# Expert layers: the row scatters of the output lose their order among each other

## The chip, the cores and the metric

The kernel runs on one core of one Trainium2 chip. The metric is the device time of one launch in microseconds (us), as the median of several runs; smaller is better. Engines are named as in the profile: PE is TensorE's matmul stream and PEld its weight loads, DVE is VectorE, ACT is ScalarE, POOL is GpSimd and SP is SyncE, which here only issues transfers.

## The reference

The first half is a gated linear attention over 4 x 8 heads of 768 steps with 48 channels each. The second half takes its 3072 output rows of 384 numbers as tokens and sends each through one of eight expert networks:

```python
def _moe_ref(x, modality_id, w_gate, modality_bias, w1, w2):
    N, D = x.shape                       # 3072, 384
    E = w_gate.shape[1]                  # 8
    logits = x @ w_gate + modality_bias[modality_id]
    e_idx = np.argmax(logits, axis=1)
    ...                                  # probs: softmax of the logits
    gate_w = probs[np.arange(N), e_idx]
    out = np.zeros((N, D), dtype=np.float32)
    for e in range(E):
        mask = e_idx == e
        h = np.maximum(x[mask] @ w1[e], 0.0)          # w1[e]: 384 x 1024
        out[mask] = gate_w[mask, None] * (h @ w2[e])  # w2[e]: 1024 x 384
    return out
```

Each token has exactly one expert, so each row of the output is written exactly once.

## The kernel before

The attention half (`gate_loop`, lines 23 to 280) fills a DRAM tensor `x_rows` with the 3072 rows in bf16 and an on-chip table `lg` with the gate logits. Beside it `cast_weights` writes bf16 copies of the expert weights, `w1b` and `w2b`, to DRAM. None of this is touched.

`moe_sorted` (lines 294 to 505) is the expert half. Lines 305 to 438 work out which expert each token goes to and give every token a slot, so that tokens of one expert stand together in tiles of 256 slots (two halves of 128). There are 12 tiles that always run and up to 7 more that run under a condition on their number (`nt`, line 499); with these inputs 13 tiles run. The table `idg` says which row of `x_rows` fills a slot, `ids` which row of `out` a slot's result goes to (an unfilled slot has an index beyond the last row, which the transfer drops).

One tile `i` goes through four functions:

- `fetch(i)`: two plain transfers on SP's queue bring the expert's weights, `w1t` (line 444) and `w2t` (line 445), 768 KB each, and two indirect transfers issued by POOL gather 128 rows each into `xg` (line 449). Weights have 3 buffers each, `xg` has 6, which is three tiles' worth of either.
- `turn`: PE transposes the gathered rows (line 457), DVE copies them to `xgT` (line 459).
- `up`: 24 matmuls into `h_ps` (line 469); the relu to `hT` is done in four pieces, two by DVE (line 471) and two by ACT (line 473).
- `down`: per half, 8 matmuls into `y_ps` (line 481), then one instruction that multiplies by the gate weight into `y_sb` (ACT for the first half, line 484; DVE for the second, line 486), then one indirect transfer issued by POOL that scatters the 128 rows of `y_sb` to `out` (line 487). `y_sb` has 4 buffers, two tiles' worth.

The written order is: fetch the next tile, `up` of this one, `turn` of the next one, `down` of this one. Every engine runs its own queue in order; the order in each queue is fixed when the kernel is built and may differ from the written one, as the gathers on POOL's queue do. Waits between instructions are derived from which tiles and tensors they read and write. A buffer of `y_sb` is written again only when the scatter that reads it has landed. All scatters write the tensor `out` at rows known only at run time, so each of them is ordered behind the one before it.

The last tile (line 505, index 12) stands in a conditional block behind line 499, which loads the number of tiles into each engine's registers.

Of the kernel before, what the change touches and what calls it, by code (L numbers as in the profile page):

```python
# [293 lines left out]
def moe_sorted(nc, ctx, tc, cpool, identb, lg, x_rows, w1b, w2b, moe_modality_id, moe_modality_bias, out):  # L294

    N, Dt = out.shape
# [140 lines left out]
    ids = mp.tile([128, NH], U32, name="ids")  # L437
# [38 lines left out]
    def down(i, w2t, hT):  # L476
        for s in range(HS):
            c = i * HS + s
            y_ps = pp.tile([128, Dt], F32, name="y_ps", tag="y", bufs=2)
            for f in range(NF):  # L480
                nc.tensor.matmul(y_ps[:], hT[:, f, s * 128:(s + 1) * 128], w2t[:, f, :], start=(f == 0), stop=(f == NF - 1))  # L481
            y_sb = fp.tile([128, Dt], F32, name="y_sb", bufs=4)
            if s % 2 == 0:
                nc.scalar.activation(y_sb[:], y_ps[:], Act.Copy, scale=inv[:, 1, c:c + 1])
            else:
                nc.vector.tensor_scalar(y_sb[:], y_ps[:], inv[:, 1, c:c + 1], None, Alu.mult)  # L486
            nc.gpsimd.indirect_dma_start(out=out, out_offset=bass.IndirectOffsetOnAxis(ap=ids[:, c:c + 1], axis=0), in_=y_sb[:], in_offset=None, bounds_check=N - 1, oob_is_err=False)  # L487


    got = fetch(0)  # L490
# [1 line left out]
    for i in range(NL):  # L492
        coming = fetch(i + 1)
        hT = up(got[0], xgT)
        if i + 1 < NL:
            xgT = turn(coming[2])
        down(i, got[1], hT)
        got = coming
    nt = nc.values_load(ntile[0:1, 0:1], min_val=NL, max_val=NS, skip_runtime_bounds_check_because="N tokens in at most E tiles that are not full")  # L499
    with ExitStack() as more:  # L500
        for i in range(NL, NS):
            more.enter_context(tc.If(nt > i))
            if i > NL:
                got = fetch(i, "n")
            down(i, got[1], up(got[0], turn(got[2])))
# [72 lines left out]
```

## Time and profile before

| | |
|---|---|
| median of 3 runs | 619.71 us (612.57 to 619.93) |
| the profiled execution, its own time | 614.6 us |
| its span, first to last instruction | 612.7 us |
| instructions | 10055 |
| PE busy | 397.7 us, 65% of the span |
| DVE busy | 354.4 us, 58% |
| ACT busy | 266.7 us, 44% |
| POOL busy | 82.7 us, 13% |
| mean granted TensorE clock | 0.851 of full |

The shares are means over the whole span, in which the attention half takes the larger part. The expert tiles begin at 482.75 us, with the first gather, and the last scatter is issued at 606.49 us. What bears on this change is read from that stretch alone.

### The profile page before, as it was taken

The numbers are of one execution on the slowest core, as the hardware profiler recorded it, in microseconds if no ns is written. First come the engines' busy times: TensorE is split into PE (matmuls) and PEld (weight loads), VectorE is DVE, ScalarE is ACT, GpSimd is POOL, SyncE is SP. The second block draws the span as 40 slices with busy tenths as digits, with TensorE's granted clock in tenths as the row PEclk, the third lists the DMA queues.
The fourth block names the chain that finished last, engine by engine and source line by source line (L and its number), as shares of the span: only waits on it lengthen the run. The fifth ranks groups of instructions, "written<-read, shape, count | busy, mean of one in ns | idle before, by whom it ended". The sixth has DMA issues, their size and how long they took to land. (4 is left out here: it accounts for less than half of the span.)

```text
span 612.7 us, 10055 instructions
## 1 busy us (share of the span) xinstructions
PE 397.7 (65%) x3656; PEld 292.1 (48%) x3656; DVE 354.4 (58%) x884; ACT 266.7 (44%) x597; POOL 82.7 (13%) x144
## 2 busy tenths in 40 slices
PE   0022122129799978987987999999914695876670
PEld 0011011117566656665656767776604574654450
DVE  1899999988876587588871444444365142232120
ACT  3556756475745574476652444444410031211120
POOL 5112000000000000000000000000000343435322
PEclk9999999999755685588996999999955599887886
DMA  9999998365652364353525445444217177765610
GB/s 201 234 243 267 261 254 218 116 175 117 172 151 74 93 159 127 87 154 99 134 70 114 88 93 105 91 98 99 50 12 305 32 269 254 255 230 184 206 53 28
DMA packets 108405, 91.49 MB, mean 149 GB/s; under 512 B 73342, under 2 KB 97314, under 8 KB 108352
## 3 DMA queue, kind: packets, MB, share of 16 engines
q1 hardware_dynamic: 93920, 70.94, 41.7%
q0 software_dynamic: 14432, 19.86, 15.7%
q8 instruction: 31, 0.51, 0.4%
q14 instruction: 22, 0.18, 0.1%
HBM read 86.75 MB, written 29.59 MB: 190 GB/s over the span
## 5 line engine op out<-in xcount | busy, mean ns | idle before, releaser
L111 PE MATMUL tq<-ident,Qh 128*96 128x128 f32 x192 | 42.9, 390 | 119.2 <-DVE Qh L107 119.2
L111 PEld LDWEIGHTS tq<-ident,Qh 128*96 128x96 f32 x192 | 31.3, 180 | 128.2 <-ACT g L76 62.0
L219 PE MATMUL py<-KW,V 96*64 96x192 f32 x512 | 88.9, 378 | 0.0
L185 DVE TENSOR_TENSOR KW<-wp,mask 96x384 f32<-96x384 f32 x64 | 35.3, 553 | 78.5 <-PE wp L184 67.0
L143 DVE TENSOR_TENSOR x<-e,an 128x192 f32<-128x192 f32 x192 | 67.7, 353 | 2.5
L184 PE MATMUL wp<-QT,KT 96*64 96x96 f32 x1024 | 65.8, 287 | 0.8 <-ACT KT L178 0.5
L184 PEld LDWEIGHTS wp<-QT,KT 96*64 96x64 f32 x1024 | 58.5, 165 | 5.6 <-ACT KT L178 4.3
L469 PE MATMUL h_ps<-xgT,w1t 128*128 128x256 bf16 x312 | 42.6, 296 | 25.2 <-DVE hT L471 22.0
L473 ACT ACTIVATE hT<-h_ps 128x512 bf16<-128x512 f32 x26 | 15.5, 597 | 97.5 <-PE h_ps L469 97.5
L150 DVE TENSOR_TENSOR e<-x 128x96 f32<-128x96 f32 x190 | 48.0, 253 | 2.7
L469 PEld LDWEIGHTS <-w1t 128*128 128x128 bf16 x312 | 32.8, 105 | 33.3 <-issue 26.3
L173 POOL MEMSET KT<- 96x256 f32 x32 | 10.9, 365 | 275.0 <-PE wp L184 275.0
L223 PE MATMUL py<-QT,Zs 96*48 96x96 f32 x448 | 37.5, 272 | 14.1 <-ACT Zs L209 14.1
L177 PE MATMUL tk<-ident,KW 96*96 96x96 f32 x256 | 40.1, 298 | 9.4 <-DMA KW<-kh 8.9
L219 PEld LDWEIGHTS py<-KW,V 96*64 96x64 f32 x512 | 39.6, 154 | 10.4 <-issue 2.4
L486 DVE TENSOR_SCALAR y_sb<-y_ps,inv 128x384 f32<-128x384 f32 x13 | 8.0, 617 | 60.9 <-DMA out_dram<-y_sb,ids 48.0
L112 ACT COPY QT<-tq 96x512 f32<-96x512 f32 x48 | 27.5, 582 | 34.9 <-PE tq L111 34.7
L481 PE MATMUL y_ps<-w2t,hT 128*128 128x384 bf16 x208 | 40.5, 353 | 0.0
L223 PEld LDWEIGHTS py<-QT,Zs 96*48 96x48 f32 x448 | 26.7, 136 | 26.9 <-ACT Zs L209 22.7
L209 ACT COPY Zs<-tz 96x512 f32<-96x512 f32 x28 | 16.3, 582 | 48.5 <-PE tz L207 48.5
L177 PEld LDWEIGHTS tk<-ident,KW 96*96 96x96 f32 x256 | 28.5, 154 | 17.6 <-issue 10.4
L178 ACT COPY KT<-tk 96x384 f32<-96x384 f32 x64 | 29.2, 477 | 16.9 <-PE tk L177 16.1
(120 smaller groups left out, 700.6 us busy)
## 6 DMA issues: line engine op xcount, KB each, us to landing
w1t<-w1b SPq DMA_DIRECT2D x13, 768.0 KB, 5.0
w2t<-w2b SPq DMA_DIRECT2D x13, 768.0 KB, 5.5
kh<-e SPq DMA_DIRECT2D x24, 384.0 KB, 2.9
KW<-kh SPq DMA_DIRECT2D x32, 288.0 KB, 3.7
w1b<-in_moe_w_dram POOLq DMA_DIRECT2D x8, 768.0 KB, 43.8
w2b<-in_moe_w_dram POOLq DMA_DIRECT2D x8, 768.0 KB, 46.4
cB<-c_scr SPq DMA_DIRECT2D x56, 96.0 KB, 3.4
ab<-in_a_re_dram SPq DMA_DIRECT2D x24, 192.0 KB, 5.3
```

Of the source, the lines that this page charges most:

```text
L111: nc.tensor.transpose(tp[:, i, :], Qh[:, t4 + i].rearrange("p c d -> p (c d)"), ident[:])
L112: nc.scalar.copy(QT[:, :, c * T + t4:c * T + t4 + 4], tp.rearrange("c t p -> c p t"))
L143: nc.vector.tensor_tensor(x[:], E[c][:, i, :, None, :].broadcast_to([P, 2, 2, D]), an[:, i].rearrange("p (u w) d -> p u w d", u=2), Alu.mult)
L150: nc.vector.tensor_tensor(to, x[:, 0], x[:, 1], Alu.add)
L177: nc.tensor.transpose(tp[:, i, :], KW[:, h4 + i, 0:C], ident[:L, :L])
L178: nc.scalar.copy(KT[:, h4:h4 + 4, 0:L], tp[:])
L184: nc.tensor.matmul(wp[u * 64:(u + 1) * 64, i, :], KT[:, h4 + i, u * 64:(u + 1) * 64], QT[:, p, :], start=True, stop=True)
L185: nc.vector.tensor_tensor(KW[:, h4:h4 + 4, C:], wp[0:L], mask[:, None, :].broadcast_to([L, 4, L]), Alu.mult)
L219: nc.tensor.matmul(py[u * 64:(u + 1) * 64, i, :], V[:, 2 * j + u, :], KW[:, 2 * j + u, :], start=True, stop=(g == 0))
L223: nc.tensor.matmul(py[u * 64:u * 64 + D, i, C:], Zs[:, j, u * 64:u * 64 + D], QT[:, p, :], start=False, stop=True)
L469: nc.tensor.matmul(h_ps[:, f, :], w1t[:, k, ff * 128:(ff + 1) * 128], xgT[:, k, :], start=(k == 0), stop=(k == KD - 1))
L481: nc.tensor.matmul(y_ps[:], hT[:, f, s * 128:(s + 1) * 128], w2t[:, f, :], start=(f == 0), stop=(f == NF - 1))
```

## The change

Each scatter is declared to have no dependence on the other members of a group named "scatter", and is then added to that group. The scatter itself, its operands, its place in the code and the number of instructions written are the same. The order between a scatter and the instruction that fills its `y_sb`, and between a scatter and the next writer of that buffer, is not part of the declaration.

```diff
@@ -484,7 +484,10 @@
                 nc.scalar.activation(y_sb[:], y_ps[:], Act.Copy, scale=inv[:, 1, c:c + 1])
             else:
                 nc.vector.tensor_scalar(y_sb[:], y_ps[:], inv[:, 1, c:c + 1], None, Alu.mult)
-            nc.gpsimd.indirect_dma_start(out=out, out_offset=bass.IndirectOffsetOnAxis(ap=ids[:, c:c + 1], axis=0), in_=y_sb[:], in_offset=None, bounds_check=N - 1, oob_is_err=False)
+
+            sc = nc.gpsimd.indirect_dma_start(out=out, out_offset=bass.IndirectOffsetOnAxis(ap=ids[:, c:c + 1], axis=0), in_=y_sb[:], in_offset=None, bounds_check=N - 1, oob_is_err=False)
+            tc.declare_no_dep(sc.ins, group="scatter", reason="rows of different tokens")
+            tc.add_to_no_dep_group("scatter", sc.ins)
```

## Rows read from the trace of the kernel before

**Rows 1.** The span in 40 slices: busy tenths of PE, POOL; granted clock.

```profile
PE   0022122129799978987987999999914695876670
POOL 5112000000000000000000000000000343435322
PEclk9999999999755685588996999999955599887886
```

**Rows 2.** Chain that ended last: start us, us, what.

```profile
600.24 2.57 DMA out_dram<-y_sb,ids
...
603.59 2.13 DMA out_dram<-y_sb,ids
...
606.49 0.97 POOL out_dram L487
```

**Rows 3.** POOL in order of time: start us, us, instruction [idle before <-releaser].

```profile
482.75 1.05 POOL L449 DMA_INDIRECT xg<-x_rows,idg  x1 [37.23 <-DVE empty L436]
...
494.17 0.95 POOL L449 DMA_INDIRECT xg<-x_rows,idg  x1 [0.30 <-PE y_ps L481]
495.42 1.03 POOL L487 DMA_INDIRECT out_dram<-y_sb,ids  x1 [0.30 <-issue]
502.66 1.00 POOL L487 DMA_INDIRECT out_dram<-y_sb,ids  x1 [6.21 <-DVE hT L471]
...
606.49 0.97 POOL L487 DMA_INDIRECT out_dram<-y_sb,ids  x1 [1.94 <-DMA out_dram<-y_sb,ids]
```

**Rows 4.** Waits, 482 to 613 us: us in total, times, longest.

```profile
DVE y_sb L486 <- DMA out_dram<-y_sb,ids: 48.0, 8, 9.0
POOL out_dram L487 <- DMA out_dram<-y_sb,ids: 30.9, 10, 5.8
PE h_ps L469 <- DVE hT L471: 22.0, 5, 6.3
```

**Rows 5.** DVE and PE around 519 us, in order of time.

```profile
519.18 0.62 DVE L486 TENSOR_SCALAR y_sb<-y_ps,inv 128x384 f32<-128x384 f32 x1 [8.96 <-DMA out_dram<-y_sb,ids]
519.72 1.28 DVE L471 TENSOR_SCALAR hT<-h_ps 128x512 bf16<-128x512 f32 x2
520.45 1.44 PE L469 MATMUL h_ps<-xgT,w1t 128*128 128x256 bf16 x6 [6.25 <-DVE hT L471]
```

**Rows 6.** PE and DVE, tiles 1 to 3 and 11, in order of time.

```profile
495.15 2.78 PE L469 MATMUL h_ps<-xgT,w1t 128*128 128x256 bf16 x24
...
495.35 0.62 DVE L486 TENSOR_SCALAR y_sb<-y_ps,inv 128x384 f32<-128x384 f32 x1 [2.04 <-PE y_ps L481]
...
500.71 2.78 PE L469 MATMUL h_ps<-xgT,w1t 128*128 128x256 bf16 x24
500.91 0.62 DVE L486 TENSOR_SCALAR y_sb<-y_ps,inv 128x384 f32<-128x384 f32 x1 [2.04 <-PE y_ps L481]
...
506.26 3.04 PE L469 MATMUL h_ps<-xgT,w1t 128*128 128x256 bf16 x24
...
581.78 2.88 PE L469 MATMUL h_ps<-xgT,w1t 128*128 128x256 bf16 x24
```

**Rows 7.** PE and DVE, end of tile 11 and tile 12, in order of time.

```profile
584.50 2.76 PE L481 MATMUL y_ps<-w2t,hT 128*128 128x384 bf16 x16
...
589.24 0.62 DVE L486 TENSOR_SCALAR y_sb<-y_ps,inv 128x384 f32<-128x384 f32 x1 [4.60 <-DMA out_dram<-y_sb,ids]
590.10 0.56 DVE L459 COPY xgT<-xg_ps 128x768 bf16<-128x768 bf16 x1 [0.24 <-DVE y_sb L486]
590.71 4.21 PE L469 MATMUL h_ps<-xgT,w1t 128*128 128x256 bf16 x24 [3.11 <-DVE xgT L459]
...
597.56 0.62 DVE L486 TENSOR_SCALAR y_sb<-y_ps,inv 128x384 f32<-128x384 f32 x1 [2.56 <-PE y_ps L481]
```

**Rows 8.** Lines 449 and 487: duration ns min/median/max; below it line 487's landing.

```profile
L449 POOL DMA_INDIRECT xg<-x_rows,idg x26: 943/962/1047, 482.8 to 574.4; - x26
L487 POOL DMA_INDIRECT out_dram<-y_sb,ids x26: 971/999/1032, 495.4 to 606.5; - x26
DMA to landing us min/median/max: 2.1/3.2/6.4
```

**Rows 9.** Stretches: us, busy by engine (x), PEclk, DMA share, GB/s.

```profile
495.00:500.50 5.50, 5.50 (x47) 4.24 (x46) 2.56 (x4) 1.78 (x3) 1.15 (x2) 1.00 0.95 337
511.90:526.30 14.40, 8.14 (x49) 5.38 (x47) 2.37 (x4) 2.36 (x4) 6.36 (x7) 0.76 0.61 209
563.90:569.40 5.50, 5.50 (x47) 4.24 (x46) 2.56 (x4) 1.19 (x2) 1.67 (x2) 1.00 0.82 264
598.20:612.70 14.50, 0.00 (x0) 0.00 (x0) 0.00 (x0) 0.00 (x0) 2.92 (x3) 0.58 0.09 30
```

**Rows 10.** SP's issues of weights: last before the expert tiles, first in them.

```profile
461.79 0.33 SPq L445 DMA_DIRECT2D w2t<-w2b  x1
492.58 0.34 SPq L444 DMA_DIRECT2D w1t<-w1b  x1
```

## The prediction

> **What bounds the kernel now.** I read the slices first, to find the stretch in which the scatters run: POOL is idle from slice 5 to slice 30 and works only in the last nine, and there PE falls from nines to sixes and lower, with its granted clock down as well [rows 1]. So PE is not what limits this stretch all the time.
>
> Then the chain of waits, to see what sets the end. It is scatter, landing, scatter: the last three are issued 3.35 and 2.90 us apart while nothing else runs [rows 2]. POOL's own timeline shows that this holds from the start. Ten gathers are issued back to back from 482.75 to 494.17 us, one every 1.27 us; then the scatters begin, and the second is issued 7.24 us after the first though its `y_sb` was written by 495.97 us [rows 3, 6] (the row blames DVE, but what was still under way was the first scatter). From the second, at 502.66, to the last, at 606.49, the 26 scatters need 103.83 us for 24 steps, 4.33 us each, 8.65 us for the two of a tile [rows 3].
>
> The table of waits tells who pays: POOL waits 30.9 us for a landing by name, DVE 48.0 us before it may write `y_sb` again, and PE 22.0 us for DVE's `hT` [rows 4]. One place shows how these hang together: DVE stands 8.96 us at line 486 for a buffer of `y_sb`; the relus of line 471 are queued behind it; PE gets `h_ps` back only then, after 6.25 us idle [rows 5]. A late scatter thus stalls DVE, DVE stalls PE, and PE comes back at the lower clock (1.44 us for 6 matmuls, against 2.78 us for 24 at full clock [rows 5, 6]).
>
> How fast the tiles go where no scatter holds them is seen at the start: the `up` matmuls of tiles 1, 2 and 3 begin at 495.15, 500.71 and 506.26 us, 5.56 us apart, at a granted clock of 1.00, the level of 2.4 GHz [rows 6, 9]. That is PE's own pace: it is busy for 5.50 of 5.50 us. Tile 11 begins at 581.78, so the ten steps from tile 1 took 86.63 us, 8.66 each [rows 6], which is the scatters' 8.65.
>
> **The change, part by part.** It adds no instruction to the work. It removes one wait for each of 25 scatters, that for the landing of the one before. What is left for a scatter is its `y_sb` and POOL's queue.
>
> *Tiles 1 to 11.* At PE's pace ten steps are 10 x 5.56 = 55.6 us against 86.63: 31.0 us less. The saving includes the clock, since the pace is that of full clock, and PE has no idle time left in which to lose it.
>
> *From tile 11 to tile 12.* Before, 590.71 - 581.78 = 8.93 us. There the last `y_sb` write of tile 11 stands ahead of `xgT` on DVE, and it waited 4.60 us for a landing [rows 7]. Without that it starts right behind the end of `down` at 584.50 + 2.76 = 587.26 (0.04 us behind, as in tile 1 [rows 6]: 500.91), takes 0.62, `xgT` follows 0.24 later, takes 0.56, and PE starts 0.05 after it: 588.77, so 6.99 us: 1.9 less.
>
> *Tile 12.* From the first `up` matmul to the end of the last `y_sb`, 598.18 - 590.71 = 7.47 us, with `up` at 4.21 us, the lower clock, after 3.11 us idle. PE would now idle about 1.2 us before it. No row shows whether the clock survives that. Bounds: nothing, or 4.21 - 2.78 = 1.4 us less. I take nothing, since the row of this very place is the nearest, and keep 1.4 for the range.
>
> *Last `y_sb` to last scatter.* Before, 606.49 - 598.18 = 8.31 us, a backlog of three scatters [rows 3, 7]. Now POOL has only its own queue: the scatter of the first half is just done, and 0.30 us lie between two of POOL's instructions, so some 0.6 us: 7.7 less. From there to the end of the span (612.7 - 606.49 = 6.2 us) nothing changes.
>
> The sum is 31.0 + 1.9 + 0 + 7.7 = 40.6 us. Against the profiled execution's own 614.6 us that gives 574. This execution lies between the runs shown, whose median is 5.1 us above it; the four times shown have a mean of 616.7, and off that I get **576 us**.
>
> **What covers what, and what is late next.** POOL: two gathers and two scatters a tile, each with 0.30 us between, are 2 x 1.26 + 2 x 1.30 = 5.12 us of 5.56 [rows 3, 8]. It is nearly full, but the gathers stand five tiles ahead of the scatters on its queue, ten being issued before the first, so a wait of a microsecond there reaches nobody.
>
> Buffers of `y_sb`: a buffer is written again two tiles later, 11.1 us. Its scatter is issued some 1.9 us after the write begins at worst (0.62 and a place in POOL's queue), lands after 6.4 us at most [rows 8], and the next instruction followed a landing by 0.78 us (600.24 + 2.57 to 603.59 [rows 2]): 9.1 us. Two microseconds are left, and this is the wait that comes back first if landings grow.
>
> The transfers: a tile moves 2 x 786 KB of weights, 2 x 98 KB of gathered and 2 x 197 KB of scattered rows, 2.16 MB. The rows allow 337 / 0.95 = 355 GB/s at a full share, in the worst of these stretches 264 / 0.82 = 322 [rows 9]: 6.1 to 6.7 us a tile, above PE's 5.56. What saves it is the lead: the weights of tiles 0 to 2 are fetched long before the first gather, and the first refill is issued at 492.58 us [rows 10]. From there up to tile 12 it is ten tiles of weights, 18 gathers (eight were issued before) and some 22 scatters, 21.8 MB. That is 61.4 us at 355, done at 554.0, and 67.7 at 322, done at 560.3; tile 12 begins at 495.15 + 55.6 + 7.0 = 557.7. So nothing to 2.6 us; I take nothing, by the first stretch, which has the fullest queues and is nearest to what is to come.
>
> The Trainium skill, page "DMA: Bandwidth & Descriptors", section "Anatomy of one DMA — SWDGE (gpsimd) path", gives the moving part of a transfer as its bytes over 436 GB/s. An estimate from that page is 5.0 us a tile, below PE's pace, so that no lead would be needed and the first rival below would fall away; the rows, at 355, do not bear that out, and I keep the rival.
>
> **The rivals.** *The transfers become the bound* (13%). For it: a share of 0.95 already in the first stretch, with less than all the scatters in it [rows 9]. Against it: the lead. If the lead doesn't help (the engines fall behind from tile 1 on, because landings of gathers and `y_sb` grow with the queues), ten steps cost up to 10 x (6.7 - 5.56) = 11.4 us; with it 2.6. That gives 579 to 588.
>
> *The scatters share what they overlap* (3%). If two scatters in flight each took twice as long to land, the pace would stay 4.33 us a scatter and the time some 617. Against it: in the last 14.5 us the share is 0.09, 1.3 us for three scatters, 0.44 us each, while each waits over 2 us to land [rows 2, 9]. A scatter is nearly all delay, and delays can overlap. [...]
>
> *The wait isn't removed* (6%): the declaration leaves an order between scatters, or another wait with the same end takes its place. Then it is some 617 us again. What speaks against it is only that the text of the change names just these instructions.
>
> *The order on POOL's queue changes for the worse* (5%, slower). The order is made anew when the kernel is built, and a scatter that no longer waits may be put ahead of gathers. If the gathers of tile i+1 come behind the scatters of tile i, a tile is a closed ring: `up` 2.78, `down` 2.76, `y_sb` 0.66, a scatter 1.30, a gather 1.26, one more gather's landing (taken as a scatter's median, 3.2), then transposes and `xgT`, some 1.1: 13.1 us a tile. Ten steps of 4.4 us more than now give 661 us. It decides as soon as the lead of five tiles falls to one; at two it costs nothing.
>
> **How the numbers follow.** The forecast has 73%: 576 us, and within it 569 (the 1.4 us of the clock, and the lowest of the times shown, 612.57 - 42.0 = 570.6, with a little room) to 582 (a microsecond or two of stalls on the highest, 619.93 - 40.6 = 579.3). The range goes up to 590 to take in the first rival; it leaves out the others, 14%. A measurement here can't tell less than about 2% from no change. Faster by more: 73 + 13 = 86%. Within 2%: 3 + 6 = 9%. Slower: 5%.
>
> **What would show it.** In the profile after, POOL's scatters should follow their `y_sb` within a microsecond or so, with no wait of theirs for a landing; the 48.0 us of DVE's line 486 should be near nothing; `up` matmuls should begin every 5.6 us to tile 11, at a clock near 1.00; the chain at the end should hold one scatter, not a row of them. The forecast is wrong if `y_sb` still waits for landings of more than 9 us, if PE waits for weights or gathers, or if the gathers' ten-deep start is gone.

## The result, and the profile after

The median of the changed kernel is 582.69 us (570.24 to 587.82, four runs) against 619.82 us (612.57 to 621.01) for the kernel before beside it; the ratio is 0.928 (95% interval 0.916 to 0.941). Two of the four executions, 587.62 and 587.82 us, are more than 1.5% above the fastest and count as slow; the ratio is that of the fast ones alone, 574.0 against 618.3 us. The forecast was 576 us, with a range of 569 to 590.

The profiled execution after took 587.82 us (span 585.8), one of the longer ones: its attention half, which the change doesn't touch, ran at a granted clock of 0.74 between 250 and 375 us (0.90 before), and the first gather came at 495.77 us against 482.75 [rows 3]. So the expert half is compared by itself, from the first gather to the end of the span: 612.7 - 482.75 = 129.95 us before, 585.8 - 495.77 = **90.03 us** after, **39.9 us less**. The forecast's sum was 40.6. Below, "the stretch" of a kernel is always this one, and a landing is the moment when an issued transfer is done.

The slices of the page after, busy tenths of PE and POOL and the granted clock, which answer to [rows 1]:

```profile
PE   0021212225979987998899799999999317899993
POOL 5111000000000000000000000000000001676731
PEclk9999999999965598576559958999999755799998
```

The scatters begin in the 35th slice. In the four whole slices behind it PE stands at 9 and the clock at 9, where [rows 1] has PE at 5 to 8 and the clock at 7 to 9, and POOL is at 6 to 7 as long as there are gathers: the same work in fewer slices. The chain that ended last, share of the span by engine, then by what it passes through:

```profile
PE 12%; issue 1%; DMA 1%; POOL 0%; POOLq 0%; DVE 0%
PE h_ps L469 6%; PE y_ps L481 5%; PE xg_ps L457 1%; DMA xg<-x_rows,idg 1%; POOL out_dram L488 0%; POOL xg L449 0%; POOLq L502 0%; DVE y_sb L486 0%; POOLq L488 0%; POOLq L503 0%
```

In place of scatter, landing, scatter [rows 2] it is matmuls, tile behind tile. POOL's own timeline (start us, us, instruction, idle before and what ended it), against [rows 3]:

```profile
495.77 1.05 POOL L449 DMA_INDIRECT xg<-x_rows,idg  x1 [37.23 <-DVE empty L436]
...
507.15 0.95 POOL L449 DMA_INDIRECT xg<-x_rows,idg  x1 [0.31 <-issue]
508.83 1.03 POOL L488 DMA_INDIRECT out_dram<-y_sb,ids  x1 [0.73 <-ACT y_sb L484]
510.17 1.00 POOL L488 DMA_INDIRECT out_dram<-y_sb,ids  x1 [0.31 <-DVE y_sb L486]
...
537.07 1.01 POOL L488 DMA_INDIRECT out_dram<-y_sb,ids  x1 [0.30 <-issue]
538.38 1.00 POOL L488 DMA_INDIRECT out_dram<-y_sb,ids  x1 [0.30 <-issue]
540.07 0.99 POOL L449 DMA_INDIRECT xg<-x_rows,idg  x1 [0.68 <-PE xg_ps L457]
541.69 0.97 POOL L449 DMA_INDIRECT xg<-x_rows,idg  x1 [0.63 <-PE y_ps L481]
...
576.83 0.97 POOL L488 DMA_INDIRECT out_dram<-y_sb,ids  x1 [4.92 <-ACTq L503]
578.10 0.97 POOL L488 DMA_INDIRECT out_dram<-y_sb,ids  x1 [0.30 <-issue]
```

The ten gathers ahead are still there, and all 26 gathers and 26 scatters stand on the queue in the order of before. The second scatter follows the first by 1.34 us where it was 7.24, and no scatter waits for a landing any more. The waits of the stretch (us in total, times, longest), against [rows 4]:

```profile
DVE y_sb L486 <- PE y_ps L481: 27.6, 13, 2.6
...
POOL out_dram L488 <- ACT y_sb L484: 9.8, 4, 3.3
...
PE h_ps L469 <- DVE xgT L459: 1.1, 1, 1.1
```

DVE's 48.0 us for a landing, POOL's 30.9 and PE's 22.0 for `hT` are gone. What DVE and POOL still wait for is the result itself; the whole of what PE waits for at line 469 is 1.1 us, before tile 12. PE in order of time, against [rows 6] and [rows 7]:

```profile
514.62 2.78 PE L469 MATMUL h_ps<-xgT,w1t 128*128 128x256 bf16 x24
...
520.17 2.78 PE L469 MATMUL h_ps<-xgT,w1t 128*128 128x256 bf16 x24
...
559.06 2.78 PE L469 MATMUL h_ps<-xgT,w1t 128*128 128x256 bf16 x24
...
564.62 2.78 PE L469 MATMUL h_ps<-xgT,w1t 128*128 128x256 bf16 x24
...
571.48 2.78 PE L469 MATMUL h_ps<-xgT,w1t 128*128 128x256 bf16 x24 [1.15 <-DVE xgT L459]
574.10 2.76 PE L481 MATMUL y_ps<-w2t,hT 128*128 128x384 bf16 x16
```

From tile 1 (509.06) to tile 11 (564.62) all ten steps are 5.55 or 5.56 us. The stretches, in the columns of [rows 9] (us, busy of PE, PEld, DVE, ACT and POOL with counts, clock, DMA share, GB/s), and line 488's durations and landings in those of [rows 8]:

```profile
509.06:564.62 55.56, 55.56 (x463) 42.50 (x461) 25.59 (x40) 17.74 (x30) 35.64 (x37) 1.00 1.01 377
564.62:578.10 13.48, 11.09 (x87) 8.09 (x85) 5.18 (x8) 3.55 (x6) 4.66 (x5) 1.00 0.22 80
578.10:585.80 7.70, 0.00 (x0) 0.00 (x0) 0.00 (x0) 0.00 (x0) 0.97 (x1) 0.70 0.02 5
514.60:520.10 5.50, 5.50 (x48) 4.24 (x46) 2.56 (x4) 1.77 (x3) 3.97 (x4) 1.00 1.02 399
```

```profile
L488 POOL DMA_INDIRECT out_dram<-y_sb,ids x26: 971/1000/1029, 508.8 to 578.1; - x26
...
DMA to landing us min/median/max: 2.1/6.0/8.9
```

PE is busy all of the 55.56 us. The DMA engines' share is 1.01 as well, at 377 to 399 GB/s, and a scatter's median landing has gone from 3.2 to 6.0 us, its longest from 6.4 to 8.9. Nothing waits for that, since the landings now overlap each other and the tiles behind them.

### The profile page after: what moved, and what is told of

It is laid out like the page before. It is cut to its first block, busy times and chain, and to the rows that moved or that the text cites. A ratio compares the mean times of both kernels' runs of the same rounds, so it can differ in the third digit from the quotient of the medians.

```text
span 585.8 us, 10054 instructions
## 1 busy us (share of the span) xinstructions
PE 401.5 (69%) x3656; PEld 297.8 (51%) x3656; DVE 356.1 (61%) x884; ACT 267.5 (46%) x597; POOL 81.8 (14%) x144
## 5 line engine op out<-in xcount | busy, mean ns | idle before, releaser
L219 PE MATMUL py<-KW,V 96*64 96x192 f32 x512 | 93.9, 399 | 0.0
L184 PE MATMUL wp<-QT,KT 96*64 96x96 f32 x1024 | 68.7, 297 | 0.7 <-ACT KT L178 0.5
L184 PEld LDWEIGHTS wp<-QT,KT 96*64 96x64 f32 x1024 | 61.2, 172 | 5.8 <-ACT KT L178 4.4
L223 PE MATMUL py<-QT,Zs 96*48 96x96 f32 x448 | 39.6, 284 | 13.9 <-ACT Zs L209 13.9
L219 PEld LDWEIGHTS py<-KW,V 96*64 96x64 f32 x512 | 42.3, 163 | 11.1 <-issue 2.4
L223 PEld LDWEIGHTS py<-QT,Zs 96*48 96x48 f32 x448 | 28.2, 143 | 27.8 <-ACT Zs L209 22.7
L469 PE MATMUL h_ps<-xgT,w1t 128*128 128x256 bf16 x312 | 38.5, 283 | 1.1 <-DVE xgT L459 1.1
L178 ACT COPY KT<-tk 96x384 f32<-96x384 f32 x64 | 29.2, 476 | 16.8 <-PE tk L177 16.1
L481 PE MATMUL y_ps<-w2t,hT 128*128 128x384 bf16 x208 | 35.9, 326 | 0.0
L229 ACT COPY yT<-py 128x192 f32<-128x192 f32 x64 | 20.4, 318 | 33.5 <-DVE state L228 28.4
L469 PEld LDWEIGHTS <-w1t 128*128 128x128 bf16 x312 | 31.6, 101 | 7.1 <-issue 1.3
```

Source lines behind the costliest of these rows:

```text
L178: nc.scalar.copy(KT[:, h4:h4 + 4, 0:L], tp[:])
L184: nc.tensor.matmul(wp[u * 64:(u + 1) * 64, i, :], KT[:, h4 + i, u * 64:(u + 1) * 64], QT[:, p, :], start=True, stop=True)
L219: nc.tensor.matmul(py[u * 64:(u + 1) * 64, i, :], V[:, 2 * j + u, :], KW[:, 2 * j + u, :], start=True, stop=(g == 0))
L223: nc.tensor.matmul(py[u * 64:u * 64 + D, i, C:], Zs[:, j, u * 64:u * 64 + D], QT[:, p, :], start=False, stop=True)
L469: nc.tensor.matmul(h_ps[:, f, :], w1t[:, k, ff * 128:(ff + 1) * 128], xgT[:, k, :], start=(k == 0), stop=(k == KD - 1))
```

## The experiments

The theory: each scatter waited for the landing of the one before, and that alone set the pace; with the waits gone PE's pace is the limit, and POOL, the buffers of `y_sb` and the transfers each have a margin, a small one. The rivals: the buffers of `y_sb` were the limit; scatters in flight share one rate; the transfers' lead is what makes it work; the gain is something else than the order.

**Many buffers, order kept.** The kernel before, with a buffer of `y_sb` for every half tile, so that DVE never waits for one.

```diff
-            y_sb = fp.tile([128, Dt], F32, name="y_sb", bufs=4)
+            y_sb = fp.tile([128, Dt], F32, name="y_sb", bufs=26)
```

> The kernel before, with 26 buffers of y_sb instead of 4: every scatter still waits for the landing of the one before, but DVE and ACT never wait for a buffer. Measure: the stretch from the first gather to the end of the span, 130.0 us before and 90.0 after the change (from the profiled executions). Theory (the row of scatters is a chain of landings, and it alone sets the pace): no gain to speak of, 120 to 135 us; the scatters still come 3.3 to 7 us apart, and PE, no longer held by y_sb, is held by gathers that stand behind scatters on POOL's queue, or finishes early and leaves a row of scatters at 3.35 us each. Rival (what costs is the stall of DVE and PE on the buffers; the chain itself is harmless): 90 to 100 us.

Measured: the stretch is 613.6 - 484.65 = 128.95 us, against 129.95; the ratio to before is 1.005 (0.998 to 1.011). From its waits, and POOL near the end:

```profile
PEld L457 <- DMA xg<-x_rows,idg: 22.9, 11, 4.4
```

```profile
601.04 0.97 POOL L487 DMA_INDIRECT out_dram<-y_sb,ids  x1 [2.36 <-issue]
604.39 0.97 POOL L487 DMA_INDIRECT out_dram<-y_sb,ids  x1 [2.38 <-DMA out_dram<-y_sb,ids]
607.31 0.97 POOL L487 DMA_INDIRECT out_dram<-y_sb,ids  x1 [1.94 <-DMA out_dram<-y_sb,ids]
```

No wait of DVE's for a buffer is left, and nothing is won. From tile 1 to tile 5 PE goes at 5.56 us a step (497.44 to 519.66); then the gathers, which stand on POOL's queue behind scatters that wait, come late, and PE waits for them instead, 22.9 us; what is not lost there is a backlog that drains at 3.35 us a scatter behind the last tile, which began at 583.15. So DVE's 48.0 us was where the cost showed, not what caused it. The chain of landings is.

**Free scatters, two buffers.** The changed kernel with half the buffers of `y_sb`.

```diff
-            y_sb = fp.tile([128, Dt], F32, name="y_sb", bufs=4)
+            y_sb = fp.tile([128, Dt], F32, name="y_sb", bufs=2)
```

> The changed kernel with 2 buffers of y_sb instead of 4: no order among scatters, but a buffer is written again one tile later, so its writer waits for the scatter of the tile before. Theory (the landing is what matters, whichever wait leads to it): a ring of write 0.62, POOL's queue 0.3 to 1.3, landing 4.8 to 6.0 and 0.8 to the next start, 7 to 8.5 us a tile against 5.56, so the stretch from the first gather to the end grows from 90 to 105 to 120 us, with DVE line 486 waiting for landings again. Rival (only the order among scatters costs): 90 to 93 us.

Measured: stretch 589.9 - 484.60 = 105.3 us, ratio 0.948 (0.935 to 0.962). From its waits:

```profile
DVE y_sb L486 <- DMA out_dram<-y_sb,ids: 24.3, 5, 6.6
```

and ACT in order of time:

```profile
503.72 0.58 ACT L484 ACTIVATE y_sb<-y_ps,inv 128x384 f32<-128x384 f32 x1 [2.57 <-DMA out_dram<-y_sb,ids]
```

The waits for landings come back at `y_sb`, the ten steps from tile 1 take 70.62 us, and still 24.7 of the 39.9 us are won. With four buffers the margin can be read from the changed kernel:

```profile
553.74 1.01 POOL L488 DMA_INDIRECT out_dram<-y_sb,ids  x1 [0.30 <-issue]
...
563.57 0.58 ACT L484 ACTIVATE y_sb<-y_ps,inv 128x384 f32<-128x384 f32 x1 [1.09 <-PE y_ps L481]
```

The scatter that took longest there was written from 552.46 us, issued at 553.74 and landed 8.9 us later, at 562.64; its buffer was written again at 563.57, 0.93 us after that, when PE's result came. How soon a waiting writer follows a landing is seen here: the scatter issued at 497.50 landed after 6.1 us, at 503.60, and ACT wrote at 503.72, some 0.1 us later. So some 0.8 us of the two microseconds that I had named were left at the worst place. My sum for it was off in three terms: the issue comes 1.28 us after the write begins and not 1.9, the landing after 8.9 and not 6.4, and the 0.78 us that I took for following a landing is POOL's, not the writer's.

**Two chains.** The order is kept among the first halves and among the second halves of tiles, and dropped between the two.

```diff
-            tc.declare_no_dep(sc.ins, group="scatter", reason="rows of different tokens")
-            tc.add_to_no_dep_group("scatter", sc.ins)
+            tc.declare_no_dep(sc.ins, group=f"half{1 - s}", reason="rows of different tokens")
+            tc.add_to_no_dep_group(f"half{s}", sc.ins)
```

> The changed kernel with two groups: the scatters of a tile's first half are ordered among themselves, and those of the second half among themselves, but not one half against the other, so that two scatters can be in flight. Theory (a scatter is nearly all delay, and delays overlap): a tile costs one landing and 0.8 us, 5.6 to 6.8 us against 5.56, so the stretch from the first gather to the end is 91 to 104 us, most of the change's gain. Rival (overlapping scatters share the engines and each takes twice as long): about 125 to 130 us, as before. Second rival (the queues are so full that landings of 8.9 us are the rule): 9.7 us a tile, 130 us.

Measured: stretch 575.5 - 481.61 = 93.9 us, ratio 0.938 (0.913 to 0.963). POOL in order of time, and from its waits:

```profile
513.56 1.00 POOL L488 DMA_INDIRECT out_dram<-y_sb,ids  x1 [0.49 <-ACT hT L473]
516.10 1.00 POOL L488 DMA_INDIRECT out_dram<-y_sb,ids  x1 [1.53 <-DMA out_dram<-y_sb,ids]
```

```profile
DVE y_sb L486 <- DMA out_dram<-y_sb,ids: 16.8, 5, 5.2
...
POOL out_dram L488 <- DMA out_dram<-y_sb,ids: 6.3, 6, 1.5
...
PE h_ps L469 <- DVE hT L471: 3.7, 3, 2.5
```

One scatter in flight beside another is enough for 36 of the 39.9 us. A landing of 5.7 us in the median (7.5 at most) stands here against one scatter of each chain in 5.56 us, so the chains hold now and then: 6.3 us of POOL's time, 16.8 of DVE's at `y_sb` behind it, and 3.7 of PE's. Tiles 1 to 11 take 59.3 us, 3.8 more than in the changed kernel.

**Two buffers for the weights.** The changed kernel with the lead of the weights cut from three tiles to two.

```diff
-        w1t = fp.tile([128, KD, F], BF16, name="w1t" + n)
-        w2t = fp.tile([128, NF, Dt], BF16, name="w2t" + n)
+        w1t = fp.tile([128, KD, F], BF16, name="w1t" + n, bufs=2)
+        w2t = fp.tile([128, NF, Dt], BF16, name="w2t" + n, bufs=2)
```

> The changed kernel with 2 buffers instead of 3 for each of the two weight tiles, so that the weights of only two tiles are on the chip before the first gather. Theory of the prediction (the transfers move 355 GB/s, slower than PE, and only the lead of three tiles hides them): one tile less of lead, and 0.55 us lost in each of ten tiles, so PE waits for weights and the stretch from the first gather to the end grows from 90 to 94 to 97 us. Rival (the transfers keep PE's pace, at 385 to 400 GB/s as in the changed kernel's trace, and landings of 6.8 us fit into the 8.3 us that two buffers leave): 90 to 92 us.

Measured: stretch 586.1 - 495.57 = 90.5 us, ratio 0.934 (0.911 to 0.957). PE in order of time:

```profile
547.89 2.79 PE L469 MATMUL h_ps<-xgT,w1t 128*128 128x256 bf16 x24
...
553.60 2.79 PE L469 MATMUL h_ps<-xgT,w1t 128*128 128x256 bf16 x24
...
559.86 2.79 PE L469 MATMUL h_ps<-xgT,w1t 128*128 128x256 bf16 x24 [0.53 <-DMA w1t<-w1b]
```

My expectation fell here: a lead of two tiles is nearly enough. The pace holds at 5.55 us to tile 7, and the next three steps take 5.74, 5.71 and 6.26; the ten steps from tile 1 lose 1.1 us against the changed kernel. The transfers run almost as fast as PE asks for them, and not at the 355 GB/s that I had worked out. A kernel with no lead at all was not run.

**More work on POOL.** The changed kernel with two small instructions on POOL behind each scatter, about 1.2 us; they compute nothing that is used.

```diff
             tc.add_to_no_dep_group("scatter", sc.ins)
+            fill = fp.tile([128, 1024], F32, name="fill", bufs=1)
+            nc.gpsimd.tensor_copy(fill[:, 0:32], y_sb[:, 0:32])
+            nc.gpsimd.memset(fill[:], 0.0)
```

> The changed kernel with idle work on POOL behind each scatter: a small copy out of y_sb (128x32) and a memset of 128x1024, some 1.3 us by the rows of the smaller memsets (96x128 in 0.2 us), no transfer and no other engine. Theory of the prediction (POOL is nearly full, 5.12 of 5.56 us a tile, so 1.5 us more a scatter makes it the bound at about 8 us a tile as long as gathers are still to be issued, tiles 0 to 7; the three tiles of gathered rows and the buffers of y_sb give back only a few us): the stretch from the first gather to the end grows from 90 to 100 to 110 us. Rival (POOL has slack, since much of what looks full is waiting): 90 to 93 us.

Measured: 585.13 us in the profiled execution, stretch 583.3 - 481.31 = 102.0 us. POOL in order of time:

```profile
524.97 1.01 POOL L488 DMA_INDIRECT out_dram<-y_sb,ids  x1 [0.30 <-issue]
525.95 0.24 POOL L492 COPY fill<-y_sb 128x32 f32<-128x32 f32 x1
526.26 0.95 POOL L493 MEMSET fill<- 128x1024 f32 x1
527.37 1.01 POOL L488 DMA_INDIRECT out_dram<-y_sb,ids  x1 [0.16 <-DVE y_sb L486]
```

POOL needs 7.40 us a tile now (a first gather at 514.99, 522.38 and 529.78), more than PE's 5.56, and becomes the bound: PE goes at its own pace for four steps (494.69 to 516.90), then the scatters come so late that `y_sb` stays occupied and DVE waits. The ten steps take 65.1 us. So POOL's 5.12 us of 5.56 is a real limit, and the changed kernel stands just under it.

**More bytes.** The changed kernel with a third plain transfer on SP a tile, 393 KB of weights that nothing reads.

```diff
+        w3t = fp.tile([128, NF // 2, Dt], BF16, name="w3t" + n)
+        nc.sync.dma_start(out=w3t[:], in_=w2b[bass.ds(te, 1), :, 0:NF // 2].rearrange("e p c d -> p (e c) d"))
```

> The changed kernel with a third weight transfer per tile on SP's queue, half of w2 once more, 393 KB that nobody reads, so 2.56 MB a tile instead of 2.16. Theory (the transfers run at what they can give in the changed kernel, 385 to 400 GB/s at a share of 1.0, and are just hidden): 6.4 to 6.7 us a tile against 5.56, less the lead of three tiles, so the stretch from the first gather to the end grows from 90 to 94 to 102 us, with PE waiting for weights. Rival (a share of 1.0 is no limit, as two queues overlap in it; there is room left): 90 to 91 us.

Measured: 582.7 us in the profiled execution, stretch 580.5 - 485.27 = 95.2 us. The number fits the theory, the mechanism doesn't. Tiles take 6.11 us while these transfers run (498.63 to 553.63, nine steps), but no row names PE waiting for weights. What is late is the second half of the relus. From the waits, and DVE in order of time:

```profile
DVE hT L473 <- PE xg_ps L459: 14.4, 8, 2.1
```

```profile
530.10 0.69 DVE L473 TENSOR_SCALAR hT<-h_ps 128x512 bf16<-128x512 f32 x1
532.56 0.69 DVE L473 TENSOR_SCALAR hT<-h_ps 128x512 bf16<-128x512 f32 x1 [1.77 <-PE xg_ps L459]
```

DVE's second relu starts 3.37 us after `up` (529.19), behind the transposes; in the changed kernel it starts 2.17 us after (539.01 and 536.84). Why it waits for the transposes here stays open, so this run says only that with three tiles of lead nine steps of 6.11 us go by without a wait for weights, at 393 GB/s on average; it doesn't give the pace at which transfers become the bound.

**All at the end.** The changed kernel with 26 buffers of `y_sb`, in which the 24 scatters of tiles 0 to 11 are held back until the last `y_sb` of tile 11 is written, by an index table `late` that depends on it.

```diff
-            y_sb = fp.tile([128, Dt], F32, name="y_sb", bufs=4)
+            y_sb = fp.tile([128, Dt], F32, name="y_sb", bufs=26)
...
+            if i < NL:
+                held.append((c, y_sb))
+            else:
+                scatter(c, y_sb, ids)
...
+    idf = mp.tile([128, NH], F32, name="idf")
+    nc.vector.scalar_tensor_tensor(idf[:], inv[:, 0, :], -1.0, empty[:], Alu.add, Alu.add)
+    late = mp.tile([128, NH], U32, name="late")
+    nc.vector.scalar_tensor_tensor(late[:], held[-1][1][:, 0:NH], 0.0, idf[:], Alu.mult, Alu.add)
+    for c, y in held:
+        scatter(c, y, late)
```

> The changed kernel with 26 buffers of y_sb in which the 24 scatters of tiles 0 to 11 are held back until tile 11 is done (their index table is written anew from the last y_sb) and then issued in a row, 16 of them before tile 12's and 8 after; no weights or gathers move beside them. It measures the disputed price by itself: the pace of scatters that may overlap, with nothing else in the queues. Theory (a scatter is nearly all delay): they are issued at POOL's pace, 1.3 us apart, and land at least as fast; the stretch from the first gather to the end is 115 to 125 us. Rival (overlapping scatters share the engines): 3.35 us apart as in the row at the end of the kernel before, 165 to 175 us.

Measured: 597.59 us in the profiled execution, stretch 595.9 - 480.80 = 115.1 us. POOL in order of time, and two stretches of scatters (columns as above):

```profile
574.87 0.98 POOL L496 DMA_INDIRECT out_dram<-y_sb,late  x1 [0.30 <-issue]
576.15 0.98 POOL L496 DMA_INDIRECT out_dram<-y_sb,late  x1 [0.30 <-issue]
```

```profile
556.80:577.10 20.30, 5.38 (x40) 3.81 (x39) 2.41 (x4) 1.78 (x3) 15.66 (x16) 0.71 0.40 147
582.30:592.40 10.10, 0.00 (x0) 0.00 (x0) 0.00 (x0) 0.00 (x0) 7.80 (x8) 0.50 0.37 136
```

Sixteen scatters in a row are issued from 556.88 to 576.15 us, 1.28 us apart, POOL's own pace; the DMA engines are at 0.40 meanwhile. In a chain, with nothing else running either, they came 3.35 us apart. Scatters do not share a rate that matters at this pace. The trace has no landing times for this kernel, so whether each also lands as fast as alone is not shown. A gap of 3.7 us lies at the second scatter of tile 12 (577.43 to 581.12), where the row names a landing; it is not settled.

By the stretch no variant is faster than the changed kernel (90.5 us at best against 90.03, one execution each). It has PE at 100%, POOL at some 5.1 us of 5.56, the DMA engines at a share of 1.01 and the buffers of `y_sb` with some 0.8 us to spare at the worst place, all at once.

## Why the prediction was right, point by point

- **What bounds the kernel now.** Right: the chain of landings. More buffers with the chain kept win nothing; two chains win 36 us.
- **Tiles 1 to 11.** Forecast 55.6 us, measured 564.62 - 509.06 = 55.56, against 86.63 [rows 6]: 31.1 us. Reading PE's free pace from the first tiles, ahead of the first held buffer, gave this term to the tenth.
- **Tile 11 to tile 12.** Forecast 6.99 us, measured 571.48 - 564.62 = 6.86, against 8.93: 2.1 us, for 1.9.
- **Tile 12.** Mis-sized: I took nothing and measured the other bound. From `up` to the end of the last `y_sb` it is 577.52 - 571.48 = 6.04 us against 7.47, 1.4 less. PE idled 1.15 us before it and kept the clock at 1.00, with `up` at 2.78 us; before, it idled 3.11 us and `up` took 4.21 [rows 7]. The row of the same place was the nearest in place, not in idle time.
- **Last `y_sb` to last scatter.** Forecast 0.6 us, measured 578.10 - 577.52 = 0.58, against 8.31: 7.7 us.
- **The tail.** Taken as unchanged at 6.2 us; it is 585.8 - 578.10 = 7.7, 1.5 longer. The last scatter now lands 3.6 us after its issue, where the same one before landed after 2.1; both spans end 4.1 us after that landing. I had forgotten that the last scatter now has another in flight, issued 1.27 us earlier.
- **The head**, first gather to tile 1, was not in the sum: 13.29 us against 12.40, with `up` of tile 0 at 5.08 us for 4.23 and a mean granted clock of 0.61 for 0.66. The variants above have 12.8 to 13.4 there, so no part of the change is to be read from it.

Together 31.1 + 2.1 + 1.4 + 7.7 - 1.5 - 0.9 = 39.9 us. That the forecast's 40.6 came so near is partly luck: three terms that I had left at nothing, 1.4, -1.5 and -0.9, add up to -1.0.

- **The whole kernel** took 582.69 us, 6.7 above the 576, of which the expert half explains little. The profiled execution, 587.82 us, had its first gather 13.0 us later than the one before; the other three left no trace. Executions of the kernel before differ as widely (610.19 to 635.25 us among the 13 beside the first four variants). I took one mean of four for it, so how near the whole time came says little; the stretch says more.
- **The transfers** as a rival: not what happened, but I argued against them for the wrong reason. I took 355 GB/s at a full share from a stretch whose share was 0.95 [rows 9], which made the lead of the weights the thing that saves it. At a share of 1.02 the engines moved 399 GB/s; a tile's 2.16 MB in 5.56 us are 388. The run with two weight buffers shows that a tile less of lead costs little. The Trainium skill, page "DMA: Bandwidth & Descriptors", section "Anatomy of one DMA — SWDGE (gpsimd) path", has 436 GB/s for the moving part; the measured rates, 377 to 401 GB/s, lie below that and above my 355. At 401, the highest of them, a tile is 5.4 us, an estimate: below PE's 5.56, as in the 5.0 us that I had worked out from the page, and not above it, as in my 6.1.
- **Scatters that share what they overlap**: fell, by the 1.28 us between scatters that were all held to the end. The overlap is not free (the median landing went from 3.2 to 6.0 us), but what is saved is the wait up to the landing, and that was most of a scatter's 3.35 us.
- **The wait isn't removed** and **the order on POOL's queue changes**: neither; POOL's timeline shows both at once.

## What to carry to other kernels

Where an engine's idle time is put down to a buffer, look at what has to land before the buffer is free, and whether that thing itself stands in a chain: more buffers for the one at the end don't help while the chain is slower than the tile. Transfers that the reader knows to be independent and the program can't are worth declaring so when they are many and each is mostly delay; here two chains in place of one already won 36 of 39.9 us. Take the new limit from a stretch of the same trace in which the old wait has not yet begun, and then go through POOL, the buffers and the transfers for the margin each has at that pace.

## What had not been expected of the hardware

A scatter issued 1.3 us behind another, with little else running, lands later than the first: the last pair of the changed kernel after 2.1 and 3.6 us, the pair before it (569.64 and 570.93) after 2.6 and 4.2. In the kernel before, one by one, the same four landed after 2.6, 2.6, 2.1 and 2.1. So a pair overlaps without being free. And a share of about 1.0 of the DMA engines stands for different rates: 377 GB/s over tiles 1 to 11, 399 in one tile of them, 401 over 510 to 547 us in the run with more bytes. In the first 50 us of the changed kernel, in the attention half, a share of 1.11 goes with 230 GB/s. So a rate divided by its share, as in my 355, is no limit.
